# Seven half-size products for an MLP's second product of two row tiles, with operand sums on GpSimd

## The chip, the cores and the metric

The kernel runs on one core of a Trainium2 chip. The metric is the device time of one execution in microseconds (us). The engines are TensorE (PE; its weight loads are shown apart as PEld), VectorE (DVE), ScalarE (ACT), GpSimd (POOL) and SyncE (SP), whose queue issues nearly all of the DMAs here. Each engine works through its instructions in the order in which the program emits them.

## The reference

Everything is fp32: 8 batches, 8 heads, 576 rows, head size 64. The first half is attention in which each row keeps its 32 highest scores; the second is a layer norm and a two-layer MLP on the heads put side by side (512 wide, 2048 hidden).

```python
scores = scale * np.matmul(q, k.transpose(0, 1, 3, 2))
kth = np.partition(scores, -top_k, axis=-1)[..., -top_k:-top_k + 1]
scores = np.where(scores >= kth, scores, -1000000000.0)
attn = np.exp(scores - np.max(scores, axis=-1, keepdims=True))
attn = attn / (np.sum(attn, axis=-1, keepdims=True) + 1e-09)
x = np.matmul(attn, v)                     # then (B,H,S,D) -> (B,S,H*D)
...
xn = (x - mu) / np.sqrt(var + 1e-06) * g_ln
out = x + np.maximum(xn @ w_ch1, 0.0) @ w_ch2
```

w_ch1 and w_ch2 arrive as 64-bit floats and are turned into fp32 early in the kernel.

## The kernel before, in words

**Units and slots.** The attention of one pair of heads and one tile of query rows is a unit: 160 in all. A batch has 576 rows, so four whole tiles of 128 rows and a rest of 64; the rests of two batches are put together to one row tile "r". The main loop runs over slots n = 0 to 165. In slot n VectorE selects the top 32 of unit n: `select` in four steps (L395, L403, L390), with `halve` of the next unit in the middle (L375 takes the maximum of the two halves of the scores; GpSimd finds the minimum, L380 and L383, which `select`'s first step of the next slot reads at L395). TensorE makes the scores of unit n + 2 at the start of the slot (L354); ScalarE copies them out (L335), masks and exponentiates an earlier unit (L430, L440); TensorE or, for "moved" units, VectorE and DMAs through HBM (L472, L477, L480) transpose the weights; `values` multiplies by v (L548, L555) and `place` brings the result into a row tile x (L587, L564).

**The MLP list.** When all heads of some row tiles are done, they become a block. Two or three row tiles make one: tiles 0 and 1 of a batch, tiles 2 and 3, and with every second batch's the tile r as a third. `add_block` decides the slot in which a block is handed in (`gives`); `give` puts its pieces on the list `todo`: turning the rows (L652, L657), 64 hidden products (L668; four of them make one part of 128 hidden units, with a relu on ScalarE at L679), then 16 second products per row tile (L684, 512 columns each, summed in one PSUM bank per tile). The evacuation at L693 scales by the layer norm's factors on ScalarE, L697 adds x on GpSimd, and the tile is stored in the next slot (L699). The rows of a new block go ahead of the last six second products of the block before it.

`fill` is called eight times in each slot. It takes pieces off the list as far as the slot's share of planned cost goes. `slot` sets this share: once the weights are converted, it is the highest constant rate at which the list still holds RESERVE = 4 us (by the planner's costs, 1.71 ns per column of a matmul) when each later block is handed in; after the last hand-over, what is left is spread over the slots that remain, and a loop behind slot 165 works off the rest. TensorE's order is thus fixed by the program, its times are not.

The hand-overs of before: slot 9 (batch 0, tiles 0 and 1), 19, 31, 44, 55, 63, 76, 83, 95, 103, 116, 123, 135, 143, 156 (batch 7, tiles 0, 1 and r) and 163 (batch 7, tiles 2 and 3); those at 44, 76, 116 and 156 have three tiles. A tile can be turned in the slot after that of its statistics (L614), when GpSimd has centred it (L620, L623).

**Memory.** w2 lies in SBUF as 16 parts of 128 hidden units by 512 columns. `mmps` has three PSUM banks for hidden and second products; `hpool` 16 tiles of 128 x 512 for the relu's results; `xpool` four tiles of two row tiles each; `rpool` one for r.

Of the kernel before, what the change touches and what calls it, by code (L numbers as in the profile page):

```python
# [9 lines left out]
AF = mybir.ActivationFunctionType  # L10
ALU = mybir.AluOpType
FP32 = mybir.dt.float32
# [9 lines left out]
J = 4  # L22
# [7 lines left out]
def kernel(  # L30
# [41 lines left out]
    nc = tc.nc  # L72
    P = nc.NUM_PARTITIONS
    B, H, S, D = q.shape
    DM = H * D
    DFF = w_ch2.shape[0]
    NC, NF = DM // P, DFF // P
    JP = J * P
    R = S - JP
# [6 lines left out]
    def pool(name, bufs, **kw):  # L86
        return ctx.enter_context(tc.tile_pool(name=name, bufs=bufs, **kw))
# [14 lines left out]
    otpool = pool("ot", 1)  # L102
    restpool = pool("ot_rest", 1)
    small = pool("small", 4)
    denpool = pool("den", 4)
    xpool = pool("x", 4)
    rpool = pool("r", 1)
    opool = pool("o", 2)
    xtpool = pool("xt", 1)
    hpool = pool("h", NF)  # L110
    hbmpool = pool("hbm", 4, space=bass.MemoryType.DRAM)
    psps = pool("ps", 5, space=PSUM)
    mmps = pool("mmps", 3, space=PSUM)

# [7 lines left out]
    def turned():  # L122
        return brief("tp")

    def product(name):
        return mmps.tile([P, 512], FP32, tag="mm", name=name)
# [120 lines left out]
    def done(step):  # L247
        return step is not None and step < now[0]

    def pop():  # L250
# [2 lines left out]
        owed[0] -= cost  # L253
        run()

    def fill(least=0):
        owed[0] = min(owed[0] + share[0], 6.0)
        while todo and (not todo[0][3] or todo[0][3]()):
            if owed[0] < todo[0][1] / 2 and least <= 0:
                break  # L260
            least -= 1
            pop()
# [122 lines left out]
    def select(u, i):  # L385

        nt = range(len(u.tiles))

        def replace(m, t, x):
            nc.vector.match_replace(x[:, t], m[:, t, :], x[:, t], LOWEST)  # L390

        if i == 0:
            for o in range(HALF, HALF + TOP_K // 2, 8):
                for t in nt:
                    nc.vector.max(u.hi[:, t, o : o + 8], u.lo[:, t])  # L395
                if o == HALF:
                    for t in nt:
                        replace(u.hi[:, :, o : o + 8], t, u.lo)
            return
        for r in ((0,), (1,), (2, 3))[i - 1]:  # L400
            m = small.tile([P, 2, 8], FP32, tag=f"m{r}", name=f"m{r}")
            for t in nt:
                nc.vector.max(m[:, t, :], u.hi[:, t])  # L403
            if r < TOP_K // 8 - 1:
                for t in nt:
                    replace(m, t, u.hi)
            if r == 0:
                u.top = m
            u.thr = m
# [189 lines left out]
    class Block:  # L599
# [38 lines left out]
            return sum(t[1] for part in self.items() for t in part)  # L638

        def items(self):  # L640
            n = self.n
            N = n * P
            xT = [None]
            hT = {}
            ps = {}

            def turn_x(i):
                if i == 0:
                    xT[0] = xtpool.tile([P, NC, 3 * P], FP32, tag="xT", name="xT")
                tp = turned()  # L650
                for c in range(NC):
                    nc.tensor.transpose(  # L652
                        tp[:, c * P : (c + 1) * P],
                        self.x[i][:, c * P : (c + 1) * P],
                        ident[:],
                    )
                nc.scalar.copy(  # L657
                    xT[0][:, :, i * P : (i + 1) * P],
                    tp[:].rearrange("p (c j) -> p c j", j=P),
                )  # L660

            def hidden(f, c):

                per = J // n if n in (1, 2) else 1
                o = f % per * N
                if c == 0 and o == 0:
                    ps["h"] = product("hps")
                nc.tensor.matmul(  # L668
                    ps["h"][:, o : o + N],
                    w1[:, c, f * P : (f + 1) * P],  # L670
                    xT[0][:, c, 0:N],
                    start=(c == 0),
                    stop=(c == NC - 1),
                )
                if c == NC - 1 and f % per == per - 1:
                    h = hpool.tile([P, J * P], FP32, tag="h", name="h")
                    for i in range(per):
                        hT[f - per + 1 + i] = h[:, i * N : (i + 1) * N]
                    nc.scalar.activation(h[:, 0 : per * N], ps["h"][:, 0 : per * N], AF.Relu)  # L679

            def project(i, f):
                if f == 0:
                    ps[i] = product("ops")
                nc.tensor.matmul(  # L684
                    ps[i][:],
                    hT[f][:, i * P : (i + 1) * P],
                    w2[:, f, :],
                    start=(f == 0),
                    stop=(f == NF - 1),
                )  # L690
                if f == NF - 1:
                    o = opool.tile([P, DM], FP32, tag="o", name="o")
                    nc.scalar.activation(  # L693
                        o[:], ps[i][:], AF.Identity,
                        bias=self.mv[:, i, 0:1], scale=self.rstd[:, i : i + 1],
                    )
                    nc.gpsimd.tensor_tensor(o[:], o[:], self.x[i], ALU.add)  # L697
                    for dst, rows in self.dsts[i]:
                        stores.append(lambda d=dst, s=o[rows, :]: nc.sync.dma_start(d, s))  # L699

            per_row = 1.71e-3
            order = [(i, f) for i in range(n) for f in range(NF)]
            if now[0] <= gives_first:

                order.sort(key=lambda x: x[1])
            return (
                [("turn", 0.44, lambda i=i: turn_x(i), lambda i=i: self.centred(i)) for i in range(n)],
                [
                    (
                        "hidden",  # L710
                        max(per_row * N, 0.31),
                        lambda f=f, c=c: hidden(f, c),
                        lambda f=f, c=c: done(ready[f * P // DM * NC + c]),
                    )
                    for f in range(NF)
                    for c in range(NC)
                ],
                [
                    (
                        "project",  # L720
                        per_row * DM,
                        lambda i=i, f=f: project(i, f),
                        lambda f=f: done(ready[NF + f]) and (f < NF - 1 or self.ready),
                    )
                    for i, f in order
                ],
            )

# [41 lines left out]
    def add_block(step, tiles, dsts):  # L772
        blk = Block(tiles, dsts)
        for i, t in enumerate(tiles):
            block_of[t] = (blk, i)
        gives.setdefault(step, []).append(blk)

    for j in jobs:
        if j.hp == NHP - 1:
            b = j.b  # L780
            step = j.last + (3 if j.last < EARLY else 4)
            tiles = [(b, qt) for g in j.groups for qt in g.qts if qt < J]
            dsts = [[(out[b, t[1] * P : (t[1] + 1) * P, :], full)] for t in tiles]
            if J in j.groups[0].qts and b % 2:

                step += 1
                tiles.append(("r", b // 2))
                dsts.append(
                    [
                        (out[b - 1, JP:S, :], slice(0, R)),  # L790
                        (out[b, JP:S, :], slice(R, P)),
                    ]
                )
            if jobs.index(j) == NHP - 1:
                step -= 1
                j.groups[0].quick = True
            if tiles:
                add_block(step, tiles, dsts)

    SLOTS = 8  # L800
    RESERVE = 4.0
# [72 lines left out]
        return max(0.0, even) / SLOTS  # L874

    recips, rows_of = {}, {}

    def arrived(n, key, x):
        blk, i = block_of[key]
        blk.x[i] = x  # L880
        rows_of.setdefault(n + 1, []).append((blk, i))
# [16 lines left out]
    for n in range(END):  # L898
# [113 lines left out]
        for x in (g, quick):  # L1012
            if x and x.job.hp == NHP - 1:
                for qt in x.qts:
                    if qt < J:
                        arrived(n, (x.job.b, qt), xs[x.job.b, qt])
        if late and late.job.hp == NHP - 1:
            r = late.job.b // 2
            arrived(n, ("r", r), rs[r])
        fill()  # L1020
    while todo or stores:
        for store in stores:
            store()
        stores.clear()
        if todo:
            pop()

# [30 lines left out]
```

## Time and profile before

Three runs took 1649.38, 1650.10 and 1651.25 us; the median is 1650.1. The profiled execution spans 1650.0 us.

| engine | busy us | share | what it does most |
|---|---|---|---|
| PE | 1555.1 | 94% | L668 hidden 554.1 us; L684 second product 546.8; L354 scores 220.5 |
| DVE | 1461.5 | 89% | L403 488.9; L390 on hi 390.7; L395 234.0 |
| ACT | 1036.4 | 63% | L440 224.8; L430 224.3; L335 199.5; relu L679 89.2 |
| POOL | 669.2 | 41% | L380 205.0; L383 204.6; L697 41.8 |

| stretch, us | PE busy | DVE busy | POOL busy | granted PE clock |
|---|---|---|---|---|
| 300 to 400 | 96.35 | 97.22 | 41.00 | 0.98 |
| 1000 to 1100 | 99.92 | 98.50 | 39.73 | 1.00 |
| 1500 to 1550 | 50.00 | 19.43 | 4.71 | 1.00 |
| 1600 to 1650 | 45.00 | 0.00 | 2.52 | 0.98 |

The DMAs move 142.28 MB; SP's queue takes 31.7% of the 16 DMA engines' time. How to read it: an engine's time is summed over the execution, so a share says nothing about which engine the others wait for; a matmul in fp32 is shown as two records, and the ends of matmuls are modelled, so durations of single records overlap and a stretch of them is read from its first start to its last end. A releaser in brackets is what the engine waited for just before that line, and how long.

### The profile page before, as it was taken

To read this page: it belongs to the slowest core of one execution; us is meant where nothing else is said; L and a number is where in the kernel's file an instruction comes from. 1 tells how busy PE (TensorE), PEld (TensorE's weight loads), DVE (VectorE), ACT (ScalarE), POOL (GpSimd) and SP (SyncE) were. 2 spreads that over 40 slices of the span, in tenths; PEclk is the share of its full clock that TensorE was granted. 3 is DMA by queue.
4 is the path that set the end of the run, shared out by engine and by line. 5 is a ranking of instruction groups with operands and counts; after the bars stand their busy time and mean duration, and the time that the engine had idled before them with its cause. 6 is when DMAs were issued, how large, how long until landed. Compare 5 with 4: busy or idle time off the path is not lost.

```text
span 1650.0 us, 24473 instructions
## 1 busy us (share of the span) xinstructions
PE 1555.1 (94%) x6825; PEld 918.2 (56%) x6825; DVE 1461.5 (89%) x4620; ACT 1036.4 (63%) x2607; POOL 669.2 (41%) x877
## 2 busy tenths in 40 slices
PE   3568999999899999999999999999999999999998
PEld 1336557566454575745547574745547575745564
DVE  5998889999999999999999999999999999997000
ACT  6887867767566665666656665667656666664310
POOL 4778753343434433343343434343343434342010
PEclk9879999999899999999999999999999999999999
DMA  7423232002342334324343335323343334222000
GB/s 178 109 86 101 66 77 53 15 14 44 80 125 85 87 107 124 98 73 101 99 131 85 87 103 129 95 75 98 103 123 93 86 93 124 88 83 72 32 13 13
DMA packets 301199, 142.28 MB, mean 86 GB/s; under 512 B 246276, under 2 KB 283144, under 8 KB 301064
## 3 DMA queue, kind: packets, MB, share of 16 engines
q1 hardware_dynamic: 296328, 140.13, 31.7%
q10 hardware_dynamic: 4736, 0.59, 0.3%
q8 instruction: 55, 0.90, 0.2%
q14 instruction: 80, 0.66, 0.1%
HBM read 93.46 MB, written 47.19 MB: 85 GB/s over the span
## 4 chain that ended last, share of the span: by engine, by line
PE 55%; DVE 32%; issue 4%; POOL 4%; ACT 3%; DMA 1%; ACTq 0%; POOLq 0%; SPq 0%; DVEq 0%
PE hps L668 21%; PE ops L684 18%; DVE m L403 10%; DVE hi L390 8%; PE scps L354 6%; DVE hi L395 5%; PE av L548 5%; DVE lo L390 3%; DVE hi L375 2%; PE tp L494 2%; PE av L555 2%; DVE sc L472 1%; POOL lo L383 1%; POOL lo L380 1%; ACT sc L335 1%
## 5 line engine op out<-in xcount | busy, mean ns | idle before, releaser
L668 PE MATMUL hps<-xT,w 128*128 128x256 f32 (+1 forms) x2048 | 554.1, 413 | 7.5 <-ACT xT L657 7.5
L684 PE MATMUL ops<-w,h 128*128 128x512 f32 x1152 | 546.8, 602 | 0.0
L403 DVE MAX8 m<-hi 128x8 f32<-128x304 f32 x1152 | 488.9, 461 | 3.3
L668 PEld LDWEIGHTS hps<-xT,w 128*128 128x128 f32 x2048 | 373.3, 192 | 125.0 <-issue 33.4
L380 POOL TENSOR_TENSOR lo<-sc,hi 128x576 int32<-128x576 int32 (+1 forms) x159 | 205.0, 1289 | 481.7 <-DVE hi L375 244.5
L390 DVE MATCH_REPLACE8 hi<-m,hi 128x304 f32<-128x304 f32 x864 | 390.7, 459 | 0.0
L684 PEld LDWEIGHTS ops<-w,h 128*128 128x128 f32 x1152 | 200.9, 191 | 186.7 <-issue 181.7
L354 PE MATMUL scps<-kT,qT 64*128 64x288 f32 (+3 forms) x1344 | 220.5, 430 | 35.6 <-DVE qT L306 25.0
L335 ACT COPY sc<-scps 128x288 f32<-128x288 f32 x576 | 199.5, 408 | 72.0 <-PE scps L354 54.8
L395 DVE MAX8 hi<-lo 128x8 f32<-128x288 f32 x576 | 234.0, 443 | 11.9 <-POOL lo L383 10.8
L430 ACT ACTIVATE e<-sc,m 128x576 f32<-128x576 f32 x288 | 224.3, 779 | 5.7 <-DVE sc L472 2.5
L440 ACT ACTIVATE e<-e,bias 128x576 f32<-128x576 f32 x288 | 224.8, 781 | 0.6
L383 POOL TENSOR_TENSOR lo<-lo,sc 128x576 int32<-128x576 int32 (+1 forms) x159 | 204.6, 1287 | 12.5
L354 PEld LDWEIGHTS scps<-kT,qT 64*128 64x128 f32 (+1 forms) x1344 | 122.7, 179 | 151.7 <-issue 56.0
L679 ACT ACTIVATE h<-hps 128x512 f32<-128x512 f32 (+1 forms) x160 | 89.2, 557 | 93.2 <-PE hps L668 92.1
L548 PE MATMUL av<-pt,vb 128*64 128x256 f32 (+2 forms) x1088 | 144.6, 409 | 0.0
L375 DVE TENSOR_TENSOR hi<-sc 128x576 f32<-128x576 f32 (+1 forms) x160 | 114.8, 718 | 13.2 <-ACT sc L335 13.1
L390 DVE MATCH_REPLACE8 lo<-hi,lo 128x288 f32<-128x288 f32 x288 | 125.5, 443 | 0.0
L697 POOL TENSOR_TENSOR o<-o,x 128x512 f32<-128x512 f32 x32 | 41.8, 1305 | 191.5 <-ACT o L693 191.5
L560 ACT COPY oT<-av 128x256 f32<-128x256 f32 (+2 forms) x68 | 26.2, 385 | 148.4 <-PE av L555 148.4
L472 DVE STREAM_TRANSPOSE sc<-e 128x512 f32<-128x512 f32 x144 | 94.2, 685 | 26.4 <-ACT e L440 26.1
L548 PEld LDWEIGHTS av<-pt,vb 128*64 128x64 f32 x1088 | 72.8, 141 | 77.4 <-ACT sc L335 13.7
(71 smaller groups left out, 1243.7 us busy)
## 6 DMA issues: line engine op xcount, KB each, us to landing
turned<-sc SPq DMA_DIRECT2D x72, 512.0 KB, 2.6
pt<-turned SPq DMA_DIRECT2D x288, 128.0 KB, 2.9
vb<-in_v_dram SPq DMA_DIRECT2D x136, 128.0 KB, 2.6
raw<-in_moe_w_ch_dram SPq DMA_DIRECT2D x32, 512.0 KB, 3.9
kin<-in_k_dram SPq DMA_DIRECT2D x128, 72.0 KB, 2.5
qin<-in_q_dram SPq DMA_DIRECT2D x120, 72.0 KB, 2.6
out_dram<-o SPq DMA_DIRECT2D x32, 256.0 KB, 2.3
ends<-in_v_dram SPq DMA_DIRECT2D x136, 16.0 KB, 2.2
```

The lines of the kernel that those rows point to most:

```text
L335: nc.scalar.copy(u.sc[:, t, s * HALF : (s + 1) * HALF], made[s][t][:, 0:HALF])
L354: nc.tensor.matmul(ps[i * R : i * R + ql, o : o + width], qT[r, q0 : q0 + ql], kT[r, k0 : k0 + width], start=True, stop=True,)
L380: nc.gpsimd.tensor_tensor(lo.bitcast(I32), a.bitcast(I32), hi.bitcast(I32), ALU.subtract)
L383: nc.gpsimd.tensor_tensor(lo.bitcast(I32), lo.bitcast(I32), b.bitcast(I32), ALU.add)
L390: nc.vector.match_replace(x[:, t], m[:, t, :], x[:, t], LOWEST)
L395: nc.vector.max(u.hi[:, t, o : o + 8], u.lo[:, t])
L403: nc.vector.max(m[:, t, :], u.hi[:, t])
L430: nc.scalar.activation(u.e[:, t], u.sc[:, t], AF.Prelu, bias=u.thr[:, t, 7:8], scale=-1.0, alpha=SLOPE)
L440: nc.scalar.activation(u.e[:, t], u.e[:, t], AF.Exp, bias=u.bias[:, t : t + 1], scale=-scale / SLOPE, accum_out=g.den[:, col : col + 1],)
L548: nc.tensor.matmul(av[h * D : (h + 1) * D, 0 : g.nq], vb[:, h * J + c, :], g.blocks[:, h, 0 : g.nq // 32, c, :], start=(c == 0), stop=False,)
L668: nc.tensor.matmul(ps["h"][:, o : o + N], w1[:, c, f * P : (f + 1) * P], xT[0][:, c, 0:N], start=(c == 0), stop=(c == NC - 1),)
L684: nc.tensor.matmul(ps[i][:], hT[f][:, i * P : (i + 1) * P], w2[:, f, :], start=(f == 0), stop=(f == NF - 1),)
```

## The change

The row tiles are regrouped and the second product of a block is computed differently.

- **Tiles.** Every block now has two row tiles. The tiles r of batches 1 and 3 make a block of their own, handed in one slot after tiles 0 and 1 of batch 3 (slot 76), those of batches 5 and 7 one at slot 156. The blocks that had r as a third tile come one slot earlier than before (43, 75, 115, 155). There are 18 blocks.
- **Second product.** The first block (`plain`) has its 32 matmuls of 512 columns as before. Each of the other 17 (`seven`) takes the two row tiles, two halves of the hidden units and two halves of the output columns as 2 x 2 blocks and forms seven products of eight matmuls with 256 columns (Strassen's scheme in Winograd's form).
- **Sums of the activations.** For each of eight tiles of hidden parts, GpSimd makes four sums or differences of 128 x 128, four fills after the relu (`SUM_LAG`).
- **Combining.** The seven products accumulate in four PSUM tiles a, b, c, d. After each product ScalarE copies 256 columns out; GpSimd adds the copies where two are needed, one fill later; then ScalarE scales the finished tile in SBUF and GpSimd adds x.
- **Forms of the weights.** After the first block's products, GpSimd makes four combinations of w2's quarters (`form_pair`, one call in each of four slots, with four operations of 128 x 512 each) and SP writes them to HBM, 4 MB. In `seven`, the right upper quarter of w2 in SBUF is a place for one form at a time: 4 slots of 256 KB. `fetch_forms`, called at the start of each `fill`, brings the next form into a slot when the matmuls that read it are behind, on SP's queue; 16 fetches per block.
- **Order.** The list entries for second products now all wait for the block's layer-norm factors (`self.ready`), and from the third product on for the forms.

The core of the diff:

```diff
-    rpool = pool("r", 1)
+    rpool = pool("r", 2)
+    tpool = pool("t", 1)
...
+    def defer(fills, run):
+        pending.append((tick[0] + fills, run))
...
     def fill(least=0):
+        tick[0] += 1
+        settle()
+        fetch_forms()
...
+        def seven(self):
...
+            def run(j, ps):
+                hs[j] = self.relu(ps)
+                waiting[j] = True
+                defer(SUM_LAG, lambda: sums(j))
...
+                a11, a21, a12, a22 = (hs[j][:, i * P : (i + 1) * P] for i in range(4))
+                s = ss[j] = hpool.tile([P, 3, P], FP32, tag="h", name="s")
+                nc.gpsimd.tensor_tensor(s[:, 0], a21, a22, ALU.add)
+                nc.gpsimd.tensor_tensor(s[:, 1], s[:, 0], a11, ALU.subtract)
+                nc.gpsimd.tensor_tensor(a21, a11, a21, ALU.subtract)
+                nc.gpsimd.tensor_tensor(s[:, 2], a12, s[:, 1], ALU.subtract)
...
+            steps = (
+                ("a", True, lambda j: part(j, 0), resident(0, 0)),
+                ("b", True, lambda j: part(j, 2), resident(1, 0)),
+                ("c", True, lambda j: ss[j][:, 0], 0),
+                ("a", False, lambda j: ss[j][:, 1], 1),
+                ("c", False, lambda j: ss[j][:, 2], resident(1, 1)),
+                ("a", False, lambda j: part(j, 1), 2),
+                ("d", True, lambda j: part(j, 3), 3),
+            )
...
+            def aside(name, *into):
+                settle(True)
+                t = tpool.tile([P, Q], FP32, tag="t", name="t")
+                copy(t[:], name)
+                return t
...
+            def evacuate(k):
+                if k == 0:
+                    for i in range(2):
+                        self.o[i] = opool.tile([P, DM], FP32, tag="o", name="o")
+                    copy(left(0), "a")
+                elif k == 1:
+                    t = aside("b")
+                    defer(1, lambda: add(left(0), left(0), t[:]))
...
+                elif k == 5:
+                    self.u = aside("a")
+                    defer(1, lambda: add(right(1), right(1), self.u[:]))
+                else:
+                    copy(left(1), "d")
+
+                    def bottom():
+                        add(left(1), left(1), self.u[:])
+                        self.finish(1)
+
+                    settle(True)
+                    defer(1, bottom)
...
+                rhs = forms(self, b, j) if isinstance(b, int) else b(j)
+                nc.tensor.matmul(
+                    bank[name][:, 0:Q], a(j), rhs,
+                    start=first and j == 0, stop=(j == G - 1),
+                    skip_group_check=not first,
+                )
...
+    def fetch_form():
+        m = fetched[0]
+        k, i = m // 4 % 4, m % 4
+        nc.sync.dma_start(
+            slot_of(i), scratch[:, k, i].rearrange("p (f n) -> p f n", f=2)
+        )
+        fetched[0] += 1
...
+    def fetch_forms():
+        may = min(seen[0] + 4, 16 * (len(blocks) - 1))
+        seen[0] = used[0]
+        if done(formed[0]):
+            while fetched[0] < may:
+                fetch_form()
...
-            if J in j.groups[0].qts and b % 2:
-
-                step += 1
-                tiles.append(("r", b // 2))
...
+            if J in j.groups[0].qts and b % 4 == 3:
+
+                add_block(
+                    step + 1,
+                    [("r", b // 2 - 1), ("r", b // 2)],
...
```

`finish` is the scaling, the addition of x and the store that stood in `project` before. The steps "0" to "3" in the last column are the forms.

## The prediction

> **What bounds the kernel now.** I read the page's strips first, then the windows, then who waits for whom, then the timeline of the end. All times are on the profiled execution: its span is 1650.0 us, the three timed runs are 1649.38 to 1651.25 (median 1650.1), so nothing has to be added around the span.
>
> ```profile
> PE   3568999999899999999999999999999999999998
> ...
> DVE  5998889999999999999999999999999999997000
> ...
> POOL 4778753343434433343343434343343434342010
> ```
> Both PE and VectorE look full from slice 5 on, but VectorE stops in slice 37 (about 1520 us), and PE goes on alone for three slices. So there are two stages with different limits, and the question is which engine sets the pace while both are full.
>
> ```profile
> engine line waited for: us in total, times, longest us
> DVE sc L472 <- ACT e L440: 7.2, 8, 2.6
> DVE hi L395 <- POOL lo L383: 3.5, 4, 1.4
> ```
> These are VectorE's waits between 440 and 1480 us: 10.7 us of 1040, and no wait for a score. Its steps repeat to 0.01 us: L375, once per unit, comes 6.90 us after the one before for many units of the same place in the batch, 8.40 for another place, 12.73 for a third. If I take the shortest gap of each place, all the excess from slot 44 to 155 is 20 us. **The middle is paced by VectorE; PE just fits under it.**
>
> ```profile
> 1494.78 6.72 PE L668 MATMUL hps<-xT,w 128*128 128x384 f32 x20 [1.06 <-ACT xT L657]
> ...
> 1589.64 27.89 PE L668 MATMUL hps<-xT,w 128*128 128x256 f32 x128
> ...
> 1617.37 27.63 PE L684 MATMUL ops<-w,h 128*128 128x512 f32 x64
> ...
> 1645.04 0.78 ACT L693 ACTIVATE o<-ops,mv,rstd 128x512 f32<-128x512 f32 x1 [12.91 <-PE ops L684]
> ...
> 1645.90 1.26 POOL L697 TENSOR_TENSOR o<-o,x 128x512 f32<-128x512 f32 x1 [12.42 <-ACT o L693]
> ```
> (An fp32 matmul has two records.) From 1494.78 PE works off the last two blocks, three row tiles and two, without a gap. Their price: 64 hidden matmuls of 256 columns take 27.6 us, 0.432 each; 32 second-product matmuls of 512 columns take 27.5, 0.859 each. The 1494.78 is also where the chain of waits passes from VectorE's pieces to PE's for good.
>
> **What the list hands to PE.** The planner spreads the list so that 4 us (RESERVE) are left when the next block is handed in. So the MLP work before the last blocks is done by then anyway, under VectorE. By its costs a block of two tiles is 56.9 us before (2 x 0.44 + 64 x 0.438 + 32 x 0.876), 53.4 after (56 x 0.438 in the last term), one of three 85.4. Slots 76 to 156 of before carry (88.9 + 6 x 56.9 + 85.4 - 4) / 80 = 6.4 us per slot; after, slots 75 to 155 carry (57.4 + 8 x 53.4 - 4) / 80 = 6.0. PE gains 0.4 us per slot of 9.3 us (735.9 us for 79 L375s), in a stage where it isn't the limit.
>
> **The parts.**
>
> Seven products: 56 x 0.432 = 24.2 us for 32 x 0.859 = 27.5, so 3.3 us per block and 56 us on PE over 17 blocks. Of these, 14 blocks lie before slot 155, under VectorE: 46 us that shorten nothing by themselves. Three lie in the end: 9.9 us.
>
> Pairing of the last rows: tile r2 is no longer done with batch 5; it comes with r3 into a block handed in at slot 156. Behind slot 155 there were 3 + 2 row tiles, now 2 + 2 + 2. This is the step that I expect to decide. The end, counted from the start of the first late hidden product:
> - Before: 1494.78 to 1645.0 is 150.2 us, of which MLP 41.6 + 41.2 + 0.9 + 27.6 + 27.5 = 138.8 (hidden of 384 columns at about 0.65), so 11.4 us are attention.
> - After: three blocks, 3 x (27.6 + 24.2) + 2 x 0.9 = 157.2. The first no longer waits for the last-row tile (whose centring ended at 1486.1); its own tiles are centred at 1477.0, and it may start in slot 156's first fill, behind that slot's scores (1481.04 now; some 1480 with less list in slot 155): + 1.2 scores, 0.9 turns, 2.6 for the six held-back matmuls = 1484.7. Attention behind that: 11.4 + 3.9 (values, placing and scores now between 1482 and 1494) = 15.3.
> - Last matmul, without new stalls: 1484.7 + 157.2 + 15.3 = 1657.2. Then before took 5.0 us to the end; after adds a 0.39 copy (L560's 128x256) and a GpSimd add of 256 columns (0.75), 1.3 with two hand-overs: 6.3. Sum 1663.5.
>
> New stalls of PE in the end, per block. Form 1 replaces form 0 in a slot that is read again six matmuls later (2.59 us), so does form 3 after form 2; form 2 has 14 matmuls. Nearest rows:
> ```profile
> vb<-in_v_dram SPq DMA_DIRECT2D x136, 128.0 KB, 2.6
> raw<-in_moe_w_ch_dram SPq DMA_DIRECT2D x32, 512.0 KB, 3.9
> ...
> out_dram<-o SPq DMA_DIRECT2D x32, 256.0 KB, 2.3
> ```
> At 2.3 us nothing is late; at 3.9 each of the two changes costs 1.4 (with 0.1 to issue), plus up to 0.5 for four 256 KB transfers per 3.46 us. I take 3.0 us, between the rows of half and double the size: 0.5 to 0.8 each. The bank of "d" is the ring's third successor of "a", so step 6 waits for ACT's copy of "a" (0.25 + 0.39 + 0.1), beside form 3's wait. Together 2 us per block, bounds 0.7 and 5: **6 us** in the end (2 to 15). 1669.5.
>
> The Trainium skill (DMA: Bandwidth & Descriptors, Anatomy of one DMA) puts a transfer, measured on GpSimd's path, at about 2.0 us plus bytes over 436 GB/s. That would be an estimated 2.6 us here, so hardly a stall but the bank's, and 1668 as the sum; this trace shows no load of this size.
>
> GpSimd in the middle. An add costs about 0.2 + 2.1 ns per column (0.215 us at 2 columns, 1.28 at 512): 0.48 for 128 columns, 32 per block, 15.4 us; four adds of 256 columns, 3.0. So 18.4 us per block of 9 slots: 2.0 us per slot, onto some 3.6 busy of 9.3 (39%). It has room; what counts is its order. L380 now waits 5 us on average for VectorE's L375, so sums queued ahead of it fit; those behind it run into the next slot's slack. The sums come four fills after their relu and should find it done. The combining adds come one fill after their copy: when queued ahead of a halving they hold L383, which has about 0.8 us of slack before L395. Before has two such GpSimd waits per block, after six: 3.5 us of lo waits x 3 = +7. Bounds 0 and +35 (1.2 us in a quarter of 112 slots).
> ```profile
> 1469.99 1.27 POOL L697 TENSOR_TENSOR o<-o,x 128x512 f32<-128x512 f32 x1 [1.95 <-ACT o L693]
> ...
> 1470.71 1.17 DVE L375 TENSOR_TENSOR hi<-sc 128x576 f32<-128x576 f32 x1
> ```
> Here VectorE's maximum took 1.17 us instead of 0.75 beside a GpSimd add: 0.42. With sums in the way at one halving in 20 that is +2 (0 to 10).
>
> The Trainium skill (SBUF — State Buffer, Who interferes with whom) speaks against the change more strongly than this one row: a VectorE instruction with two SBUF inputs is locked out for the whole of a GpSimd instruction that reads SBUF, at every meeting. By the rule a sum in progress costs on average half its 0.48 us; if sums ran at a third of 112 halvings the term would be 9 us and the sum 1678.
>
> Fetches in the middle: 272 of 256 KB, 71 MB, on SP's queue:
> ```profile
> SPq L477 <- DVE hi L395: 427.8, 61, 13.9
> SPq L480 <- DMA turned<-sc: 167.3, 70, 3.8
> ```
> (waits of SP's queue, 200 to 1500 us) SP often stands still for a move (7 us each), and a fetch behind it comes late by up to 6 us. Behind a waiting fetch stand the moves, their reads and the loads. PE then falls behind, up to about a slot, before VectorE misses a score; its 0.4 us per slot pay 3.7 us per block. I take 0, bounds 0 and +25 (3 us per block in 8 blocks). Copies on ACT: 7 x 0.39 = 2.7 us per block, where it is 63% busy: nothing; but the copy into the single tile t waits for GpSimd's add that frees it, and behind it stand the score copies and the exps: in B's price. The 16 adds for the forms (21 us over four slots) and their 16 stores come once, at slots 21 to 24: 0 to 5, taken as 0.
>
> Gain in the middle: at most the 20 us of excess. The 7.2 us of waits for e can go when PE, and ACT behind it, are earlier: -7. Middle: +7 + 2 - 7 = +2. **Sum 1669.5 + 2 = 1671.**
>
> **Rivals.**
> A, the above, 1654 to 1690: 0.59.
> B, GpSimd's and SP's queues reach VectorE: lo late in many slots, forms late behind moves. For it: L383's slack is under 1 us. Against it: GpSimd is idle half the time. 1671 + 20 to 55, some 1700: 0.17.
> C, faster: the relief of PE takes all 20 us of excess off VectorE's steps, and forms arrive in 2.3 us. 1663.5 + 2 - 20 = 1645, and with PE 3 us less behind at slot 155, 1642. It decides where what the middle gives exceeds the 13.5 us of the longer end plus its stalls. For it: with 6.2 us per slot (slots 55 to 75) PE was about 4 us less behind. Against: only 10.7 us of VectorE's waits are seen. If PE were the limit after all, up to 46 us would go, about 1625; the missing score waits speak against that. 0.15.
> D, between: within 0.2% (about what a measurement of this kernel can tell from no change; 1646.8 to 1653.4): 0.09.
> That the seven products bring PE nothing, since weight loads double per column, is excluded by the 256-column hidden products: the load takes 0.19 us and hides under 0.216.
>
> **Numbers.** 1671. Leaving out C's lower part and B's upper part: 1643 to 1705. Faster 0.15, same 0.09, slower 0.76.
>
> **What would show it.** Right: VectorE's last halving stays within 10 us of 1503.6, its waits from 440 to 1480 under 30 us; the late hidden products start near 1485 and PE works alone for some 20 us longer; in the end PE waits under 1 us for each of two form changes per block. Wrong: halvings move earlier by over 15 us (C), waits of L395 for L383 or of PE for forms above 40 us in all (B), or the end isn't longer than before.

## The result and the profile after

The changed kernel takes 1754.3 us (median of four runs, 1751.76 to 1755.76) against 1650.2 (1649.38 to 1651.25): a ratio of 1.0628, 95% interval 1.0613 to 1.0643. The forecast of 1671 and its range up to 1705 were too low. The profiled execution of after spans 1749.9 us, 99.9 more than that of before.

The strips of the page, after:

```profile
PE   2678989999888989899899988989998999999987
...
DVE  5998898999899999889899989798989899983000
```

PE has nearly the same busy time as before (1559.6 us against 1555.1, though the seven products need fewer columns), but both strips that were solid nines now have holes, and VectorE stops in slice 37 again, but a slice is 43.7 us now instead of 41.2. The time divides in two. VectorE's last halving (L394, L375 before) moved from 1503.6 to 1575.3 us: **71.7 us were lost in the middle.** From there to the end it was 146.4 us and is 174.6: **28.2 in the end.**

VectorE's waits, after, 300 to 1576 us (us in total, times, longest):

```profile
DVE sc L492 <- ACT e L460: 42.7, 24, 5.4
DVE hi L414 <- POOL lo L402: 39.6, 19, 9.1
```

In the same stage of before (300 to 1504 us) these two came to 7.2 and 7.8. So VectorE now waits 82.3 us instead of 15.0. It waits for no score here, as before. From 250 us on, two thirds of its slots (95 of 136) take what they take without fetches to 0.02 us, and about one per block is 3 to 9 us longer. PE's and SP's waits over the whole span of after:

```profile
PE ops L869 <- DMA w<-forms: 90.3, 38, 6.9
```
```profile
SPq L932 <- PE ops L869: 293.9, 130, 33.1
SPq L497 <- DVE hi L414: 199.7, 38, 13.8
SPq L500 <- DMA turned<-sc: 184.4, 70, 4.5
```

PE waits for fetches of forms, 38 times and 2.4 us each on average. SP waits at fetches (L932) for PE, at moves (L497) for VectorE, and at the reads of moves (L500) for the DMAs before them. All stand in one queue. The fetches on the page (how many, size of each, median us from issue to landing):

```profile
w<-forms SPq DMA_DIRECT2D x272, 256.0 KB, 3.2
```

One event shows how a late fetch reaches VectorE through lo. The timeline of after, 1080 to 1106 us (start, duration, instruction; in brackets the idle time before and its releaser):

```profile
1082.80 1.78 SPq L500 DMA_DIRECT2D pt<-turned  x4
...
1084.68 7.68 SPq L932 DMA_DIRECT2D w<-forms  x6
...
1087.97 2.93 PE L869 MATMUL ops<-w,s 128*128 128x256 f32 x6 [4.56 <-DMA w<-forms]
...
1091.15 0.52 ACT L584 ACTIVATE r<-xo,dr 128x64 f32<-128x64 f32 x2 [5.97 <-PE xo L614]
...
1096.17 0.37 ACT L818 COPY t<-ops 128x256 f32<-128x256 f32 x1 [1.52 <-PE ops L869]
...
1096.62 0.73 POOL L827 TENSOR_TENSOR o<-o,t 128x256 f32<-128x256 f32 x1 [12.61 <-ACT t L818]
...
1099.52 1.27 POOL L682 TENSOR_TENSOR o<-o,x 128x512 f32<-128x512 f32 x1 [2.16 <-ACT o L678]
1100.74 0.80 POOL L399 TENSOR_TENSOR lo<-sc,hi 128x288 int32<-128x288 int32 x1
...
1102.44 0.46 DVE L414 MAX8 hi<-lo 128x8 f32<-128x288 f32 x1 [9.10 <-POOL lo L402]
```

The fetch stands behind four reads of a move, is issued from 1084.68 on and lands some three us later; PE waits 4.56 us for it. ScalarE stands in order behind PE's results (5.97 and 1.52). GpSimd has gone to its combining add (L827) and waits 12.61 us there for ScalarE's copy, then 2.16 more at the addition of x to the finished tile (L682). The first step of the minimum for VectorE's next `select` (L399) stands behind both, although its input was ready when the halving at 1088.85 had ended; VectorE waits 9.10.

The way through e, in the same timeline at 843 to 851 us:

```profile
843.70 1.13 PE L869 MATMUL ops<-w,h 128*128 128x256 f32 x4 [1.18 <-DMA w<-forms]
...
846.26 0.37 ACT L818 COPY o<-ops 128x256 f32<-128x256 f32 x1 [3.15 <-PE ops L869]
...
849.31 0.76 ACT L460 ACTIVATE e<-e,bias 128x576 f32<-128x576 f32 x1
...
850.19 0.71 DVE L492 STREAM_TRANSPOSE sc<-e 128x512 f32<-128x512 f32 x1 [5.45 <-ACT e L460]
```

ScalarE waits 3.15 us for a product whose matmuls waited for forms (1.18 here, 4.06 at 835.63); the exp that VectorE needs stands behind that copy in its order, and VectorE waits 5.45.

In the end, PE's and SP's timeline of after, the first late hidden product and the last block's last form:

```profile
1552.72 4.48 PE L700 MATMUL hps<-xT,w 128*128 128x256 f32 x20
...
1678.31 2.08 PE L869 MATMUL ops<-w,h 128*128 128x256 f32 x4 [4.39 <-DMA w<-forms]
...
1731.31 3.62 PE L869 MATMUL ops<-w,h 128*128 128x256 f32 x16
1738.30 5.28 PE L869 MATMUL ops<-w,h 128*128 128x256 f32 x16 [3.37 <-DMA w<-forms]
```
```profile
1734.95 0.36 SPq L684 DMA_DIRECT2D out_dram<-o  x1
1735.40 1.96 SPq L932 DMA_DIRECT2D w<-forms  x4
```

The eight matmuls at 1731.31 read form 2. The first slot is free after two of them, at about 1732.2 (a quarter of 3.62 us), but on SP's queue the store of the block's first tile stands ahead of the fetch and waits for GpSimd, so the fetches of form 3 start at 1735.40. The eight matmuls after the wait take 5.28 us, the eight before it 3.62.

### The profile page after: what moved, and what is told of

The parts are those of the page before. It is cut to its first block, busy times and chain, and to the rows that moved or that the text cites. A ratio compares the mean times of both kernels' runs of the same rounds, so it can differ in the third digit from the quotient of the medians.

```text
span 1749.9 us, 27740 instructions
## 1 busy us (share of the span) xinstructions
PE 1559.6 (89%) x7897; PEld 1146.4 (66%) x7897; DVE 1463.3 (84%) x4620; ACT 1067.7 (61%) x2712; POOL 971.6 (56%) x1509
## 4 chain that ended last, share of the span: by engine, by line
DVE 46%; PE 26%; POOL 10%; DMA 8%; ACT 5%; issue 2%; SPq 2%; DVEq 0%; ACTq 0%; POOLq 0%
DVE m L423 14%; DVE hi L409 12%; PE ops L869 11%; DVE hi L414 7%; PE hps L700 7%; DMA w<-forms 5%; DVE lo L409 4%; DVE hi L394 3%; DVE sc L492 3%; PE scps L373 3%; POOL lo L402 2%; POOL lo L399 2%; PE av L568 2%; DMA turned<-sc 2%; ACT sc L354 1%
## 5 line engine op out<-in xcount | busy, mean ns | idle before, releaser
L700 PE MATMUL hps<-xT,w 128*128 128x256 f32 x2304 | 557.9, 387 | 3.0 <-ACT xT L671 3.0
L700 PEld LDWEIGHTS hps<-xT,w 128*128 128x128 f32 x2304 | 422.8, 193 | 82.5 <-issue 26.4
L399 POOL TENSOR_TENSOR lo<-sc,hi 128x576 int32<-128x576 int32 (+1 forms) x159 | 204.5, 1286 | 270.9 <-DVE hi L394 150.9
L869 PE MATMUL ops<-w,h 128*128 128x256 f32 x1088 | 282.3, 400 | 41.9 <-DMA w<-forms 41.8
L869 PE MATMUL ops<-w,s 128*128 128x256 f32 x816 | 218.4, 409 | 48.8 <-DMA w<-forms 48.6
L869 PEld LDWEIGHTS ops<-w,s 128*128 128x128 f32 x816 | 157.1, 204 | 88.2 <-DMA w<-forms 51.9
L827 POOL TENSOR_TENSOR o<-o,t 128x256 f32<-128x256 f32 x68 | 50.6, 744 | 222.2 <-ACT t L818 136.2
L568 PE MATMUL av<-pt,vb 128*64 128x256 f32 (+2 forms) x1088 | 150.1, 419 | 9.8 <-DMA pt<-turned 5.3
L723 ACT ACTIVATE h<-hps 128x512 f32<-128x512 f32 x144 | 86.5, 600 | 71.2 <-PE hps L700 70.4
L568 PEld LDWEIGHTS av<-pt,vb 128*64 128x64 f32 x1088 | 75.5, 143 | 75.8 <-issue 21.1
```

Source lines behind the costliest of these rows:

```text
L399: nc.gpsimd.tensor_tensor(lo.bitcast(I32), a.bitcast(I32), hi.bitcast(I32), ALU.subtract)
L568: nc.tensor.matmul(av[h * D : (h + 1) * D, 0 : g.nq], vb[:, h * J + c, :], g.blocks[:, h, 0 : g.nq // 32, c, :], start=(c == 0), stop=False,)
L700: nc.tensor.matmul(ps[0][:, side * N : (side + 1) * N], w1[:, c, f * P : (f + 1) * P], self.xT[:, c, 0:N], start=(c == 0), stop=(c == NC - 1),
L869: nc.tensor.matmul(bank[name][:, 0:Q], a(j), rhs, start=first and j == 0, stop=(j == G - 1), skip_group_check=not first,)
```

## The experiments

The theories: **L**, forms land late and PE's waits for them pass on through ScalarE and GpSimd; **G**, GpSimd's added sums and adds delay the minimum by themselves. All ratios are to before.

**No fetches.**
```diff
-        nc.sync.dma_start(
-            slot_of(i), scratch[:, k, i].rearrange("p (f n) -> p f n", f=2)
-        )
```


> The changed kernel without the 272 fetches of forms (four of the seven products then read whatever the quarter of w2 holds, so that part of the product is not computed). Theory L (late forms: a fetch stands on SP's queue behind moves, stores and loads, PE waits for it, ScalarE's copies wait with PE, and the exponentials and the halving's minimum come late for VectorE): most of VectorE's 65 us of new waits go, and PE's form waits in the end: 1670 to 1695, VectorE's waits from 440 to 1550 us under 30. Theory G (GpSimd's sums and combining adds, waiting in its own queue, hold the minimum and the biases): only PE's 12 us of form waits in the end and the slow clock behind them go: 1730 to 1742.

1655.4 us, ratio 1.0027 (1.0016 to 1.0037). VectorE's waits, 300 to 1492 us:
```profile
DVE hi L414 <- POOL lo L402: 3.5, 7, 1.2
```
Nearly everything hangs on the fetches, more than L itself had said. All sums, adds and copies are still there, and the waits for e and lo are below those of before.

**No sums on GpSimd.**
```diff
-                nc.gpsimd.tensor_tensor(s[:, 0], a21, a22, ALU.add)
...
+                ss[j] = hs[j][:].rearrange("p (k n) -> p k n", n=P)
```


> The changed kernel without GpSimd's four sums per hidden part (544 small operations; the products read the relu's parts instead, so the sums of activations are not computed); fetches, combining adds and everything else as they are. Theory L: GpSimd has the room, 1735 to 1752. Theory G: 1680 to 1715.

1752.6, ratio 1.0619 (1.0596 to 1.0643), 0.6 above L's range and far from G's. GpSimd's busy time falls from 971.6 to 737.0 us and the time stays. G falls: the sums do not matter here, and the combining adds, which this run keeps, cost nothing without fetches.

**Pairing alone**, in the kernel before.
```diff
-    rpool = pool("r", 1)
+    rpool = pool("r", 2)
...
-            if J in j.groups[0].qts and b % 2:
...
+            if J in j.groups[0].qts and b % 4 == 3:
```


> The kernel before with the pairing of the last-row tiles alone (blocks at 43, 75, 76, 115, 155, 156; all products as before). The prediction's step: two row tiles more behind slot 155 less what lay there, now without the seven products' 9.9 us: 5 x 28.1 before, 6 x 28.1 after, one slot earlier; 1650 + 11.4 + 9.9 = 1671 (1664 to 1676), the middle unchanged. Rival, that the pairing costs nothing because the middle carries less: 1650 within 4.

1662.8, ratio 1.0082 (1.0066 to 1.0099), below the expected interval. The last halving comes at 1495.5 and the end after it takes 164.8 us: 18.4 longer than before's 146.4, while the middle is 8 us shorter, which the expectation had as unchanged. VectorE's waits do not explain that (14.2 us, 15.0 before); why is open.

**Alternating order.** Between two products that read forms stands one that reads a resident quarter, so a fetch has the time of eight more matmuls. The copies and adds move with the products.
```diff
             steps = (
+                ("d", True, lambda j: part(j, 3), 0),
                 ("a", True, lambda j: part(j, 0), resident(0, 0)),
+                ("c", True, lambda j: ss[j][:, 0], 1),
                 ("b", True, lambda j: part(j, 2), resident(1, 0)),
...
```


> The changed kernel with the seven products in another order (form 3, quarter, form 0, quarter, form 1, quarter, form 2), so that a product with a quarter that stays in SBUF lies between every two forms and a slot has 14 matmuls instead of 6 until it is read again; the result is the same. Theory L: the waits for forms fall by half or more, and VectorE's with them: 1690 to 1720. Theory G: 1745 to 1760.

1694.0, ratio 1.0271 (1.0254 to 1.0287): 60 us of the 104 come back by an order alone. PE's waits, whole span:
```profile
PE ops L868 <- DMA w<-forms: 29.9, 18, 4.1
```

**Fetches on ScalarE's queue**, in the order of the change, and then with the alternating order.
```diff
-        nc.sync.dma_start(
+        nc.scalar.dma_start(
```


> The changed kernel with the 272 fetches issued on ScalarE's queue instead of SP's; everything else the same. Two readings of the late forms: L1, the place in SP's queue (behind moves that wait for VectorE and for their own transfer, behind loads and stores) makes them late; L2, the transfer itself (3.2 us to land, against 2.6 us of PE work between two readings of a slot). L1: PE's waits for forms fall from 90 us to under 35, less ScalarE's some 0.45 us per issue (7 us per block on an engine 61% busy): 1675 to 1710. L2: the waits stay over 65 us, 1730 to 1765.

> The order of the products of the run with alternating forms, and the fetches on ScalarE's queue. L1: hardly a wait for forms, 1655 to 1675. L2: as with alternating forms alone, 1685 to 1700.

1757.6, ratio 1.0649 (1.0633 to 1.0665), and 1726.2, ratio 1.0466 (1.0448 to 1.0483). The first lies in L2's range, in time and in waits (70.8 us), but doesn't part the theories: the fetches now stand among ScalarE's own instructions, which wait for PE too (79.6 us at L818 for products). The second is in neither range: PE waits 5.7 us for forms, as L1 had said, but the time is 26 us above L2's. PE's longest waits from 300 to 1500 us are now for transfers of the moved units:
```profile
PE av L568 <- DMA pt<-turned: 30.1, 7, 6.6
PE av L568 <- DMA dr<-den: 20.9, 4, 7.3
```
In the alternating order on SP's queue these are 7.2 and 8.0, and VectorE's waits for e double, from 10.7 to 21.3 (in W, below). That a fetch waiting for PE holds the exps behind it in ScalarE's order would fit; no view shows it.

**The same transfers to elsewhere.** All 272, at the same places of SP's queue, but from HBM to HBM, so that no product waits for them.
```diff
-            slot_of(i), scratch[:, k, i].rearrange("p (f n) -> p f n", f=2)
+            aside_in_hbm[:, k, i].rearrange("p (f n) -> p f n", f=2),
+            scratch[:, k, i].rearrange("p (f n) -> p f n", f=2),
```


> The changed kernel with the same 272 transfers from the same place in HBM, at the same places in SP's queue, but written to another place in HBM instead of w2's quarter: SP's work and the bytes read stay, PE neither waits for them nor holds them up (the four products read what the quarter holds, so the form products are not computed). If PE's waits are the price: 1650 to 1662, as without fetches. Rival, the transfers and SP's time delay moves, loads and stores: 1675 and above, with VectorE's waits over 40 us.

1664.3, ratio 1.0083 (1.0067 to 1.0098), 2 us above the first range and far below the rival's, although each lands only after 4.6 us. VectorE's waits are 13.6 us. In this form, bytes and SP's issuing cost 9 us over no fetches; the other 90 come with the waits between fetches and products. (The profile puts three waits of PE at L568, 17.2 us, down to these transfers, whose tile it does not read; why is open.) What the writing into SBUF costs by itself was not run; the small fetches, below, bound it.

**Seven products, alternating, in the last three blocks only.**
```diff
-            return self.plain() if self is blocks[0] else self.seven()
+            return self.seven() if self in blocks[-3:] else self.plain()
```


> Seven products (alternating order) for the last three blocks alone, which are worked off when VectorE is done; all other blocks with the plain second product; tiles paired as in the change. If PE's saving counts where PE is alone: the pairing's 1662.8 less 9.9, plus 1.3 for the longer combination, plus 0 to 3 for forms: 1655 (1651 to 1659). Rival, the half-size products save nothing: 1663 or above.

1670.5, ratio 1.0119 (1.0104 to 1.0134): a miss, in the rival's range. The end, from the last halving at 1504.4 on, takes 164.8 us, as with pairing alone. PE's timeline:
```profile
1604.82 2.07 PE L668 MATMUL tp<-ident,x 128*128 128x128 f32 x8 [3.60 <-POOL x L643]
```
The rows of the last block now wait for GpSimd, where a combining add that waits for ScalarE's copy and the addition of x stand ahead of their centring. The turns take 2.07 us here (1.04 at 1614.63 in the end of after) and the twelve records behind them 0.9 longer. But the rival's reason is not what the trace shows: the 9.9 us that PE saves in three blocks are spent, 3.6 on this wait, 1.9 on the longer turns and matmuls, 1.5 on one wait for a form and 2.0 on the last steps (7.0 us from the last matmul to the end, 5.0 with pairing alone); 0.9 stays open. The middle was 8.9 us longer than with pairing alone, 6.1 of it in waits (W below: 20.3, all for lo, against 14.2); why is open.

**Small fetches**: 16 partitions of each, 32 KB instead of 256, so most of each form is not renewed.
```diff
-            slot_of(i), scratch[:, k, i].rearrange("p (f n) -> p f n", f=2)
+            slot_of(i)[0:16], scratch[0:16, k, i].rearrange("p (f n) -> p f n", f=2)
```


> The changed kernel with each fetch cut to 16 of 128 partitions (32 KB instead of 256), at the same places in SP's queue and with the same waits; the form products then use old data in the other partitions and are not computed. So far the time is that without fetches (1655), 9 us for transfers and SP's work, and PE's waits for forms one for one (90 us). L1, the place in SP's queue: most of the waits stay, 55 to 85 us, 1705 to 1740. L2, size and landing of 256 KB: under 30 us, 1665 to 1690.

1720.7, ratio 1.0425 (1.0404 to 1.0446). Issues on the page, then PE's waits:
```profile
w<-forms SPq DMA_DIRECT2D x272, 32.0 KB, 1.8
```
```profile
PE ops L869 <- DMA w<-forms: 68.9, 25, 5.9
```
In L1's range, in time and waits. With an eighth of the bytes and 1.4 us less to land, three quarters of PE's waits remain; the time falls by 33.6 us. Most of PE's waiting is for a late start, not a long flight; size, flight and the writing into SBUF together are worth about a third of the 104 us.

**Fetch at once**: emitted right behind the matmul that last reads the slot, in the order of the change and in the alternating one.
```diff
                 if isinstance(b, int) and j % 2:
                     used[0] += 1
+                    seen[0] = used[0]
+                    fetch_forms()
```


> The changed kernel with each fetch emitted right behind the matmul that read its slot last, up to two fills (about 2 us) earlier in SP's order, so ahead of more moves and loads. L1: form waits 35 to 65 us, 1700 to 1730. L2: unchanged, 1745 and above.

> Alternating order of forms and fetches emitted at once; the result is the same. L1: hardly a form wait (under 12 us), 1662 to 1678. L2: as with the alternating order alone, 1688 to 1700.

1774.2, ratio 1.0761 (1.0733 to 1.0789), and 1708.7, ratio 1.0353 (1.0337 to 1.0369): both later, where L1 had said earlier; the first is in L2's range, the second above both. PE's waits for forms are 95.8 us (90.3 in after) and 26.1 (29.9 in the alternating order). SP's waits of the first:
```profile
SPq L934 <- PE ops L869: 341.4, 138, 33.5
```
SP now stands 47.5 us longer at fetches for PE, and what is queued behind a fetch, moves too, cannot be issued meanwhile; how much of the 20 us comes by that was not split. So L in its simple form (fetches come late because they are emitted late) falls: on this queue, early is as bad as late.

**Alternating, one fill later.**
```diff
-        seen[0] = used[0]
+        seen[:] = [seen[1], used[0]]
```


> The seven products with the alternating order (form, quarter, form, quarter, ...), as in the run that took 1694, but each fetch of a form is put on SP's queue one filling call later than there. Theory S (in the alternating order the remaining waits come from SP standing at the fetches for PE, 157 us of SP's waits between 440 and 1530 us, which holds the moves, loads and stores behind them): SP's waits for the products fall below 60 us, PE's waits for forms stay under 35 us because a whole resident product lies between two forms, and the time falls to 1670 to 1688. Theory F (what remains is fetches that land late behind other transfers on the queue): a later fetch only lands later, PE's waits for forms rise above 35 us, and the time is 1694 or more, up to 1715.

1715.8, ratio 1.0406 (1.0383 to 1.0429). PE's, then SP's waits, 440 to 1530 us:
```profile
PE ops L868 <- DMA w<-forms: 41.7, 16, 6.1
```
```profile
SPq L931 <- PE ops L868: 146.3, 77, 11.0
```
S is wrong: SP's waits for products stay (157.3 in the alternating order at the change's own place, 146.3 one fill later), and PE's waits for forms rise, as F said; the time is 0.8 above F's range. In the alternating order the change's own place is the best of the three that were tried.

**All together.** W is the sum of VectorE's waits for e, lo and scores from 300 us to its last halving, H the time of that halving.

| kernel | time us | PE's waits for forms | W | H | H - W |
|---|---|---|---|---|---|
| before | 1650.2 | - | 15.0 | 1503.6 | 1488.6 |
| no fetches | 1655.4 | 0 | 3.5 | 1491.5 | 1488.0 |
| pairing alone | 1662.8 | - | 14.2 | 1495.5 | 1481.3 |
| to elsewhere | 1664.3 | 0 | 13.6 | 1503.7 | 1490.1 |
| last three blocks | 1670.5 | 1.5 | 20.3 | 1504.4 | 1484.1 |
| alternating | 1694.0 | 29.9 | 35.3 | 1527.8 | 1492.5 |
| alternating, at once | 1708.7 | 26.1 | 48.2 | 1542.2 | 1494.0 |
| alternating, later | 1715.8 | 45.5 | 49.6 | 1542.0 | 1492.4 |
| small | 1720.7 | 68.9 | 48.9 | 1545.4 | 1496.5 |
| alternating, ScalarE's queue | 1726.2 | 5.7 | 54.9 | 1548.3 | 1493.4 |
| no sums | 1752.6 | 99.1 | 87.2 | 1573.8 | 1486.6 |
| after | 1754.3 | 90.3 | 82.3 | 1575.3 | 1493.0 |
| ScalarE's queue | 1757.6 | 70.8 | 75.9 | 1569.0 | 1493.1 |
| at once | 1774.2 | 95.8 | 111.0 | 1606.8 | 1495.8 |

H goes over 115 us and H - W over 15 (1481 to 1497): the middle is VectorE's own work plus its waits for e and lo, whatever the seven products save on PE. PE's waits for forms price the kernel only roughly. 1664.3 + 29.9 is 1694.2 and 1664.3 + 90.3 is 1754.6, both within 0.3 us of the runs; by the other runs that is luck. Small lies 12 and no sums 11 us below such a sum; alternating, later lies 6 above, at once 14, alternating, at once 18, and the two on ScalarE's queue 23 and 56. No kernel with all of the reference's work in it beat the kernel before; the nearest, pairing alone, has 1662.8.

## Why the prediction was wrong

**The step that failed** is "Fetches in the middle", of which the prediction said "I take 0, bounds 0 and +25". The row for it was shown there: SP's 427.8 us of waits at moves. The text concluded that a fetch comes up to 6 us late, that PE then falls behind, "up to about a slot, before VectorE misses a score", and that PE's savings pay it back. VectorE indeed misses no score. It is reached by two other ways, which leave no such slack: e through ScalarE, which copies PE's products out in order ahead of its exps, and lo through GpSimd, which waits at a combining add for such a copy. (The working did see exps behind a copy, but only for a copy that waits for GpSimd, and put it into B's price.) Their waits from 300 us on, 42.7 and 39.6, are 67.3 us more than before's 15.0, of the middle's 71.7. No fetches takes them away; a changed order, size or place of the fetches moves H and W together.

**The making of the forms** was taken as 0, with bounds 0 and 5. It cost 7.7 us, once: from the halving at 240.19 to that at 293.76 after takes 53.6 us, the same five slots of before (243.32 to 289.19) 45.9. This lies ahead of the 300 us from which W counts; without fetches it is there too, and made up for later.

**Rival B** had the mechanism, its name and its sign ("PE for forms above 40 us in all": 90.3), but a chance of 0.17 and a price of 20 to 55, where 83 were wanted (1754.3 less 1671). The largest price that the fetches of the middle had in the working was 3 us per block in 8 blocks; PE's waits for forms ahead of the end are 79.2 us (90.3 less 11.1), 5.7 per block in 14 blocks.

**Queues were asked in one direction only.** "Behind a waiting fetch stand the moves" was written and given no price. At once, where SP stands there 47.5 us longer, is 20 us slower.

**GpSimd's order** was taken at +7, with bounds 0 and +35. By itself it costs nothing: without fetches, lo waits are 3.5 us. Its adds matter only as carriers of PE's delays. The operations' costs were right: a sum takes 0.46 us (0.48 forecast), a combining add 0.74 (0.75).

**VectorE beside GpSimd**: +2 forecast. The halvings take 113.5 us in all after, 112.5 without the sums and 114.8 before, so at most 1 us. By the rule of the Trainium skill (SBUF — State Buffer, Who interferes with whom) the prediction had an estimated 9, for sums running at a third of the halvings. Read one by one in the trace of after, only 10 of the 128 whole halvings meet a sum; four of these take 0.79 to 0.94 us, the other six 0.75, as those do that meet nothing. Before, 9 of the 12 that met the longer L697 took 0.83 to 1.66. So single meetings do cost, as the rule says, but not all, and with the sums they are rare.

**The end** was nearly right. From the first late hidden product at 1552.72 to the last matmul at about 1743.6 it is 190.9 us; forecast were 157.2 + 15.3 + 6 = 178.5. Waits for forms are 11.1 instead of 6. The runs of matmuls behind such waits take 5.7 more, against rows of the same count elsewhere in the end: 1.7 in the sixteen records at 1738.30, 2.7 from 1678.31 to 1685.3 (the turns among them), 0.6 at 1598.97 and 0.75 at 1723.65. The rest, 1.6, stays open. The last matmul to the end took 6.3, as forecast. The mis-sized terms were the wait, and the longer runs of matmuls behind it, which had no term. In the wait it was not the flight of 3.0 us (3.2 measured), but what stands ahead of it on SP, twice a store and once the reads of a move; form 1's change cost 0.18 and 0.25 in two of the blocks, form 3's 2.90, 4.39 and 3.37. The Trainium skill (DMA: Bandwidth & Descriptors, Anatomy of one DMA) gives, by a fit for GpSimd's path, an estimated 2.6 us for 256 KB and 2.1 for 32 KB; on SP's queue this case has 3.2 and 1.8.

**What held:** the middle is paced by VectorE, so PE's 46 us there bring nothing (H - W); the first late hidden product was forecast at 1484.7 for an undelayed middle, and came 68.0 us later, with VectorE's 71.7; pairing lengthens the end, by 18.4 us. And rival C is excluded as the seven products stand: even without fetches the middle gains 12.1 us at most (1491.5 for 1503.6), and the end takes 12.4 back (158.8 for 146.4).

## What to carry to other kernels

When a DMA waits for one engine and is queued among transfers that wait for another, the two engines are coupled in both directions; price each such pair per event, and follow a late transfer through every in-order engine behind it to the one that sets the pace, not only along the obvious operand. Saved work on an engine that isn't the limit buys no slack if the same change makes that engine wait. If such fetches can't be avoided, other work between two uses of the buffer is worth more (60 us here) than earlier issue, a smaller transfer or another busy queue.

## What was not expected of the hardware

The granted clock of TensorE falls around a single wait within full work. After, 1080 to 1100 us in steps of 5 (busy time and instructions by engine, then granted clock, DMA share, GB/s):

```profile
1080.00:1085.00 5.00, 3.32 (x18) 2.10 (x18) 4.76 (x16) 3.32 (x10) 2.65 (x4) 1.00 0.55 194
1085.00:1090.00 5.00, 2.03 (x5) 1.67 (x6) 5.00 (x19) 0.19 (x1) 0.00 (x0) 0.61 0.87 262
1090.00:1095.00 5.00, 5.00 (x19) 4.05 (x18) 3.34 (x13) 1.16 (x4) 0.00 (x0) 0.71 0.53 138
1095.00:1100.00 5.00, 5.00 (x29) 3.80 (x28) 0.00 (x0) 3.80 (x12) 1.21 (x2) 1.00 0.59 198
```

Around the wait of 4.56 us the clock is 0.61 and in the next 5 us 0.71, with PE busy all that time: ten records of 256 columns that take 2.32 us at 1099.02 take 3.33 at 1090.91. In windows of 2 us the clock is 1.00 up to 1086, then 0.53, 0.50, 0.50 and 0.76, and 1.00 again from 1094 on: it is halved while PE still waits and stays so for some 5 us of full work. So some 2.4 us follow the wait: 1.4 in the six records at 1087.97 (2.93 us, 1.56 at 1097.18) and 1.0 in these ten. The mean clock of the profiled execution is 0.950 after, 0.981 before, 0.970 without fetches. What sets it off is open: no run changed a wait alone.
